# Retention in a fused kernel: one chunk per visit in every group, or two chunks in every second group

## The chip, the cores and the metric

One core of a Trainium2 chip runs the kernel. The metric is the device time of one execution in microseconds; the median of three runs of the kernel before is 662.99 us (662.89 to 663.08).

## The reference, cut to what matters

A retention layer runs over q, k, v of shape (4, 8, 768, 64): batch, heads, time, head dimension. Its output, rearranged to 3072 tokens of 512, goes through a feed-forward block with 2048 hidden columns.

```python
for t in range(S):
    state = gamma[None, :, None, None] * state + np.einsum('bhd,bhe->bhde', k[:, :, t], v[:, :, t])
    y[:, :, t] = scale * np.einsum('bhd,bhde->bhe', q[:, :, t], state)
x = y.transpose(0, 2, 1, 3).reshape(B * S, H * D)
h = x @ w_in
sp = np.maximum(h, 0.0) + np.log1p(np.exp(-np.abs(h)))
out = (h * erf(sp)) @ w_out
```

## The kernel before, in words

**Retention in chunks.** Time is cut into chunks of 128 steps: 6 per batch, 24 in all, numbered j (j % 6 is the place in the batch). Keys and queries are scaled by powers of gamma, so that the state needs no decay between chunks. A chunk needs its scores (keys times queries inside each half chunk of 64 steps), the causal mask on them, the masked scores times the values, the old state times the queries, the crossed part of the second half, and two additions to the state, one per half chunk. Heads are 64 wide, so all of these are 64x64 matmuls, which use the quadrants of TensorE's array; all else on TensorE is 128x128.

**The feed-forward block.** The first 512 tokens (groups g = 0 to 3, `hidden` at L865, `project` at L885) are computed in the plain way, while the weights are still being converted from 64-bit words. From group G0 = 4 on the work goes by 256 tokens, two groups to each: g - G0 even and odd hold the two halves of the hidden columns. Group G0 takes the plain product (`hidden_plain`, L971); the groups from G0+1 to G0+19 use a scheme with 26 products in place of 32 for the hidden columns (`hidden_steps`, L942: 26 steps of two matmuls, whose results VectorE and ScalarE add up from four PSUM banks, two named hp and two named r) and 7 in place of 8 for the output (`project_part`, L1022). The scheme wants sums of x (`x_sums`, L921: 18 VectorE operations for each 256 tokens), sums of weights (`W_SUMS`, `sums` at L347, whose additions are DMAs issued by POOL) and sums of the gated values (`g_sums`, L1004).

**The order of a group** is written out by hand in the loop at L1224. Each engine executes its part in this order. TensorE does the 26 steps of group g with products 1, 2 and 4 of group g-1 set behind steps 14, 18 and 24; then a visit to the retention, `sub_visit` (L713), one chunk in each group from G0 (j = 6) to G0+17 (j = 23); then products 5, 6, 7 and 3 of group g-1. ScalarE computes softplus of the hidden values, copies the visit's results to xT, then computes erf. VectorE does the additions and masks of the visit, then x_sums (in odd groups) or the preparation of a chunk (in even ones, `prepared` at L533: scale the keys, scale and transpose the blocks of keys and queries), then the gate `gated` (L846), h times erf. The results of a pair of groups are added up and written out in the next odd group (`put_part`, L1048, from four PSUM banks o0 to o3).

**A visit** (L713 to L797) multiplies the old state with the queries, adds the products of keys and values for both half chunks into two banks (`adds`), multiplies values with the masked scores, straight and crossed, makes the scores of the next chunk, and then multiplies the state after the first half with the queries. VectorE adds to the state between (L777) and behind (L797). Chunk 6 is an exception: its scores and its first half's addition are made in the middle of `hidden_plain` (`sub_begin`, L708).

**Transfers.** `load` (L192) brings a chunk's keys in rows, its queries and keys once more as blocks that VectorE can transpose (`load_blocks`, L181: 16 transfers each) and its values: 34 transfers, all issued by SP, behind the visit. The results of the first 512 tokens go out through SP too (`put_first`, L907).

Of the kernel before, what the change touches and what calls it, by code (L numbers as in the profile page):

```python
# [19 lines left out]
P = 128  # L20
C = 128
# [115 lines left out]
def kernel(  # L137
# [39 lines left out]
    KQ, V, KB = {}, {}, {}  # L177
# [3 lines left out]
    def load_blocks(to, src):  # L181


        for s, d in itertools.product(range(2), range(2)):
            part = slice((2 * s + d) * 32, (2 * s + d + 1) * 32)
            for u in range(HP):
                nc.sync.dma_start(
                    to[part, u * C : (u + 1) * C].rearrange("p (a d) -> p a d", d=32),
                    src[2 * u + s, :, d * 32 : (d + 1) * 32].rearrange("(a p) d -> p a d", p=32),
                )  # L190

    def load(j):  # L192
        b, c = divmod(j, NC)
        if j == JPC - 1:

            x = act.tile([P, N], F32, name="e", bufs=1)
            KQ[j] = x[:, : 2 * d_model].rearrange("p (i h d) -> p i h d", i=2, h=H)
            V[j] = x[:, 2 * d_model : 3 * d_model].rearrange("p (h d) -> p h d", h=H)
        else:
            KQ[j] = loads.tile([P, 2, H, D], F32, name="kq")  # L200
            V[j] = loads.tile([P, H, D], F32, name="v")
        now = slice(c * C, (c + 1) * C)
        if j >= NB:
            KB[j] = loads.tile([P, HP * C], F32, name="kb", bufs=2)
            nc.sync.dma_start(KQ[j][:, 0], k[b, :, now, :].rearrange("h p d -> p h d"))
            load_blocks(KQ[j][:, 1].rearrange("p h d -> p (h d)"), q[b, :, now, :])
            load_blocks(KB[j], k[b, :, now, :])
        for i, src in enumerate((k, q) if j < NB else ()):
            nc.sync.dma_start(KQ[j][:, i], src[b, :, now, :].rearrange("h p d -> p h d"))
        if not early:  # L210
            load_values(j)

    def load_values(j):
        b, c = divmod(j, NC)
        nc.sync.dma_start(V[j], v[b, :, c * C : (c + 1) * C, :].rearrange("h p d -> p h d"))

# [214 lines left out]
    state_2 = loads.tile([P, HP * C], F32, name="kb", bufs=2)[:, : HP * D]  # L431
    state_2 = state_2.rearrange("p (u d) -> p u d", d=D)
    mid = [state, state_1, state_2, state, None, state_1]
    adds_of = {JPC: range(2), JPC + 1: range(1), JPC + 2: range(1)}
# [97 lines left out]

    def prepared(j):  # L533

        if j >= NJ:
            return
        nc.vector.tensor_tensor(
            KQ[j][:, 0], KQ[j][:, 0],
            kq_s[:, j % NC, 0, :, None].to_broadcast([P, H, D]), op=ALU.mult,
        )  # L540
        yield
        blocks = (KB[j], KQ[j][:, 1].rearrange("p h d -> p (h d)"))
        for i, x in enumerate(blocks):
            x = x.rearrange("p (u a d) -> p u a d", u=HP, d=32)
            by = kq_b[:, j % NC, i, :, :, None].to_broadcast([P, HP, 4, 32])
            nc.vector.tensor_tensor(x, x, by, op=ALU.mult)
            yield
        for name, store, x in zip("kq", (KT, QT), blocks):
            store[j] = ret.tile([P, HP, C], F32, name=name + "T")
            nc.vector.transpose(store[j].rearrange("p u t -> p (u t)"), x)  # L550
            yield
# [161 lines left out]
    def sub_visit(j, g):  # L713
# [8 lines left out]
        pp = [ret_psum() for _ in range(2)]  # L722
# [7 lines left out]
        def of_state(a):  # L730
            t = slice(a * D, (a + 1) * D)
            for u in PAIRS:
                for r in range(2):
                    col, own = u // 2, slice(r * D, (r + 1) * D)
                    x = state_1 if g == G0 else state
                    nc.tensor.matmul(  # L736
                        pp[r][col * D : (col + 1) * D, u % 2, t], x[own, u, :], QT[j][own, u, t],
                        start=first(r, col), stop=True, skip_group_check=True,
                    )

        other = SC[j + 1] = [ret_psum(ps_h) for _ in range(2)]

        def of_values(crossed):
            for u in PAIRS:
                for a in range(2):
                    r = 1 - a if crossed else a
                    col, t = u // 2, slice(a * D, (a + 1) * D)
                    own = slice(col * D, (col + 1) * D)  # L750
                    nc.tensor.matmul(  # L751
                        other[a][own, u % 2, D:] if crossed else pp[a][own, u % 2, t],
                        V[j][t, 2 * u + r, :],
                        AM[j][t, r, u, :D],
                        start=crossed or first(r, col), stop=True, skip_group_check=True,
                    )

        if c:
            of_state(0)
        last = chunk_of(g - 1)  # L760
        if (g - G0) % 2 == 1:
            clear.update((("o", 0), ("o", 1)))
        new = [
            None if g == G0 else O[last][3][:, 1, :].rearrange("p (u d) -> p u d", d=D),
            pp[1][:, 2:, :].rearrange("p a (b d) -> p (a b) d", d=D),
        ]
        adds = range(int(g == G0), 2 if c < NC - 1 else 1)
        for u in range(HP):
            for r in range(2):
                for a in adds:  # L770
                    t, h = slice(a * D, (a + 1) * D), 2 * u + r
                    nc.tensor.matmul(  # L772
                        new[a][r * D : (r + 1) * D, u, :], KQ[j][t, 0, h, :], V[j][t, h, :],
                        start=first("o" if a == 0 else 1, r), stop=True, skip_group_check=True,
                    )
        if g > G0 and c:
            nc.vector.tensor_tensor(state, state, new[0], op=ALU.add)  # L777
        elif g > G0:
            nc.vector.tensor_copy(state, new[0])
        of_values(False)  # L780
        of_values(True)
        if j + 1 < NJ:
            sub_scores(j + 1)
            sub_mask(j + 1)
        of_state(1)
        for r in range(2):
            a = 1 - r
            x, y = XC[m][:, r::2, i * C : (i + 1) * C], other[a][:, :2, D:]
            if c or a:
                nc.scalar.copy(x, pp[r][:, :2, :])  # L790
                x = x[:, :, a * D : (a + 1) * D]
                nc.vector.tensor_tensor(x, x, y, op=ALU.add)
            else:
                nc.scalar.copy(x[:, :, D:], pp[r][:, :2, D:])
                nc.scalar.copy(x[:, :, :D], y)
        if c < NC - 1:
            nc.vector.tensor_tensor(state, state_1 if g == G0 else state, new[1], op=ALU.add)  # L797
# [109 lines left out]
    def put_first(tt):  # L907
        o = E[G0 - 1].rearrange("p (u t c) -> p t u c", u=FG, t=TT)[:, tt]
        nc.scalar.copy(o, O[0][tt].rearrange("p (u c) -> p u c", u=FG))
        nc.sync.dma_start(out[tt * P : (tt + 1) * P, :].rearrange("p (u c) -> p u c", u=FG), o)  # L910
# [109 lines left out]
    HOME = {2: (0, 0), 6: (0, 1), 5: (1, 0), 7: (1, 1), 3: (2, 0), 4: (2, 1), 1: (3, 0)}  # L1020

    def project_part(g, p, at=slice(None)):  # L1022
# [7 lines left out]
        i, half = (3, 1) if p == 4 and g >= NG - 2 else HOME[p]  # L1030
# [17 lines left out]
    def put_part(m, step):  # L1048


        o26, o57, o34, o1 = (O[m][i] for i in range(4))
        if step == 0:
            R[m] = act.tile([P, 8, DH], F32, name="r", bufs=1)
            nc.scalar.copy(R[m][:, 7], o1[:, 0])
            return
# [11 lines left out]
        else:  # L1067
            nc.vector.tensor_tensor(r[:, 1:3], r[:, 5:7], o34, op=ALU.add)
# [37 lines left out]
    def next_scores():  # L1106
# [37 lines left out]
            ([(load, 6), (sub_results, 5)], []),  # L1144
            ([(load, 7)], [(sub_sums, 5)]),
# [40 lines left out]
    j = JPC + 2  # L1186
    sum_in(1, 12)
    all_of(prepared(j))
    load(j + 2)
    gated(G0 - 1)  # L1190
    for n, _ in enumerate(hidden_plain(G0), start=1):
        if n in (1, 4, 7):
            next(last_steps)
        if n == 3:
            sub_begin(j)
    sum_in(1, 20)
    x_sums(G0)
    sub_states(j)
    all_of(prepared(j + 1))
    sum_in(1, len(W_SUMS))  # L1200
# [3 lines left out]
    sub_visit(j, G0)  # L1204
    load(j + 3)
# [3 lines left out]
    sum_in(0, 12)  # L1209
    for tt in range(1, TT):  # L1210
# [4 lines left out]
    j += 1  # L1215
# [8 lines left out]
    for g in range(G0 + 1, NG):  # L1224
# [6 lines left out]
        next_chunk = prepared(j + 1) if even or put is None else iter(())  # L1231

        if put is not None:
            order = {18: (e_sums,), 20: (e_sums,), 24: (e_sums, e_sums)}
        else:
# [4 lines left out]
        if g == G0 + 1:  # L1240
            order.update({n: (w_sums,) for n in (1, 2, 3, 4)})
# [12 lines left out]
        all_of(next_chunk)  # L1254

        nc.scalar.activation(idle, idle, AF.Softplus)
        gate_softplus(g)
        if more:
            sub_visit(j, g)
        all_of(w_sums)  # L1260
        if g == G0 + 1:
            all_of(last_steps)
        if g + 1 < NG and not even:
            x_sums(g + 1)
        if more:
            if even:
                all_of(prepared(j + 2))
            if j + 3 < NJ:
                load(j + 3)
            j += 1  # L1270
        gate_erf(g)
        for p in (5, 6, 7, 3):
# [77 lines left out]
```

## Time and profile before

| what | value |
|---|---|
| median of 3 runs | 662.99 us |
| the profiled execution | 662.78 us |
| its span, first to last instruction | 660.9 us |
| granted TensorE clock | 1.00 |
| TensorE matmul busy | 655.7 us, 6200 instructions |
| VectorE busy | 508.4 us |
| ScalarE busy | 280.2 us |
| transfers | 51.88 MB, 159413 packets |

The span runs from the first to the last instruction; 1.9 us of the execution lie around it. A float32 matmul call of the kernel stands as two instructions in the trace. A row of the timeline names start, length, engine, line, operation, tiles, shape and number of instructions; idle time ahead of it and what ended that stand in brackets. A matmul's length there includes its way through the array; how fast matmuls follow one another is read from their starts. The hidden stages of the groups G0+1, G0+2, G0+3 begin at 158.41, 184.32 and 210.25 us, that of the last group at 622.07 us.

### The profile page before, as it was taken

The numbers are of one execution on the slowest core, as the hardware profiler recorded it, in microseconds if no ns is written. First come the engines' busy times: TensorE is split into PE (matmuls) and PEld (weight loads), VectorE is DVE, ScalarE is ACT, GpSimd is POOL, SyncE is SP. The second block draws the span as 40 slices with busy tenths as digits, with TensorE's granted clock in tenths as the row PEclk, the third lists the DMA queues.
The fourth block names the chain that finished last, engine by engine and source line by source line (L and its number), as shares of the span: only waits on it lengthen the run. The fifth ranks groups of instructions, "written<-read, shape, count | busy, mean of one in ns | idle before, by whom it ended". The sixth has DMA issues, their size and how long they took to land.

```text
span 660.9 us, 15247 instructions
## 1 busy us (share of the span) xinstructions
PE 655.7 (99%) x6200; PEld 557.3 (84%) x6200; DVE 508.4 (77%) x1102; ACT 280.2 (42%) x402; POOL 11.7 (2%) x29
## 2 busy tenths in 40 slices
PE   8999999999999999999999999999999999999998
PEld 7744444576999999999999999999999999999997
DVE  5999999969986786788678678677687688476464
ACT  3468363445534334244254253342432542533440
POOL 1000000110100000000000000000000000000000
PEclk9999999999999999999999999999999999999999
DMA  9999844385753321222222322221231210000000
GB/s 188 223 264 231 211 129 107 63 152 90 144 123 61 85 47 32 67 47 46 70 44 47 73 39 46 42 72 37 44 79 36 46 53 1 2 34 0 1 33 32
DMA packets 159413, 51.88 MB, mean 78 GB/s; under 512 B 143216, under 2 KB 149744, under 8 KB 159344
## 3 DMA queue, kind: packets, MB, share of 16 engines
q1 hardware_dynamic: 157776, 46.72, 32.8%
q0 software_dynamic: 1152, 4.19, 3.4%
q8 instruction: 48, 0.79, 0.5%
q14 instruction: 21, 0.17, 0.1%
q10 hardware_dynamic: 416, 0.01, 0.0%
HBM read 40.39 MB, written 6.29 MB: 71 GB/s over the span
## 4 chain that ended last, share of the span: by engine, by line
PE 98%; DMA 1%; DVE 0%; ACT 0%; issue 0%
PE o L1034 37%; PE hp L951 22%; PE r L951 12%; PE hp L860 8%; PE o L896 8%; PE hp L980 2%; PE r L736 2%; PE hp L628 1%; PE o L772 1%; PE r L524 1%; PE r L557 1%; PE o L604 1%; PE r L751 1%; PE hp L751 1%; DMA kq<-in_k_dram 1%; PE r L772 0%
## 5 line engine op out<-in xcount | busy, mean ns | idle before, releaser
L1034 PE MATMUL o<-w_out_sb,h 128*128 128x256 f32 (+1 forms) x640 | 142.7, 380 | 0.0
L951 PE MATMUL hp<-xs,w_in_sb 128*128 128x128 f32 x988 | 138.1, 275 | 0.0
L1034 PEld LDWEIGHTS o<-w_out_sb,h 128*128 128x128 f32 x640 | 119.5, 190 | 16.6
L963 DVE TENSOR_TENSOR h<-h,hp 128x256 f32<-128x256 f32 x190 | 78.0, 418 | 70.5 <-PE hp L951 65.6
L951 PEld LDWEIGHTS hp<-xs,w_in_sb 128*128 128x128 f32 x988 | 128.4, 192 | 3.0
L1034 PE MATMUL o<-w_out_sb,e 128*128 128x256 f32 x480 | 113.5, 379 | 0.0
L1034 PEld LDWEIGHTS o<-w_out_sb,e 128*128 128x128 f32 x480 | 86.8, 190 | 9.4
L817 ACT ACTIVATE e<-h 128x2048 f32<-128x2048 f32 x22 | 42.1, 1912 | 119.6 <-DVE h L963 119.6
L963 DVE TENSOR_TENSOR h<-h,r 128x256 f32<-128x256 f32 x152 | 56.9, 415 | 22.3 <-PE r L951 21.4
L965 ACT COPY h<-hp 128x256 f32<-128x256 f32 x38 | 14.2, 373 | 130.7 <-PE hp L951 122.7
L951 PE MATMUL r<-xs,w_in_sb 128*128 128x128 f32 x456 | 63.3, 275 | 0.0
L951 PEld LDWEIGHTS r<-xs,w_in_sb 128*128 128x128 f32 x456 | 57.0, 192 | 0.0
L860 PE MATMUL hp<-xT,w_in_sb 128*128 128x512 f32 (+2 forms) x144 | 56.5, 548 | 0.0
L849 DVE TENSOR_TENSOR e<-h,e 128x1024 f32<-128x1024 f32 x42 | 49.2, 1213 | 8.0 <-ACT e L830 8.0
L860 PEld LDWEIGHTS hp<-xT,w_in_sb 128*128 128x128 f32 x144 | 25.8, 190 | 27.0 <-issue 24.6
L951 PE MATMUL hp<-xT,w_in_sb 128*128 128x128 f32 x304 | 46.3, 275 | 0.0
L951 PEld LDWEIGHTS hp<-xT,w_in_sb 128*128 128x128 f32 x304 | 41.5, 192 | 1.4 <-issue 0.5
L830 ACT ACTIVATE e<-e 128x2048 f32<-128x2048 f32 (+1 forms) x23 | 42.1, 1836 | 0.2
L967 ACT ACTIVATE h<-hp 128x256 f32<-128x256 f32 x57 | 21.9, 384 | 29.7 <-PE hp L951 28.3
L951 PE MATMUL r<-xT,w_in_sb 128*128 128x128 f32 x228 | 31.7, 275 | 0.0
L830 ACT ACT_TABLE_LOAD x24 | 30.8, 1283 | 0.4
L951 PEld LDWEIGHTS r<-xT,w_in_sb 128*128 128x128 f32 x228 | 28.5, 192 | 0.0
(164 smaller groups left out, 799.0 us busy)
## 6 DMA issues: line engine op xcount, KB each, us to landing
w_out_sb<-in_moe_w_out_dram SPq DMA_DIRECT2D x14, 512.0 KB, 5.2
kq<-in_k_dram SPq DMA_DIRECT2D x23, 256.0 KB, 4.0
v<-in_v_dram SPq DMA_DIRECT2D x23, 256.0 KB, 3.4
out_dram<-r SPq DMA_DIRECT2D x23, 256.0 KB, 2.9
kq<-in_q_dram SPq DMA_DIRECT2D x288, 16.0 KB, 1.9
kb<-in_k_dram SPq DMA_DIRECT2D x288, 16.0 KB, 1.8
w_in_sb<-in_moe_w_in_dram SPq DMA_DIRECT2D x8, 512.0 KB, 10.1
w_out_sb<-w_out_sb POOLq DMA_DIRECT2D x8, 512.0 KB, 5.3
```

Of the source, the lines that this page charges most:

```text
L736: nc.tensor.matmul(pp[r][col * D : (col + 1) * D, u % 2, t], x[own, u, :], QT[j][own, u, t], start=first(r, col), stop=True, skip_group_ch ...
L751: nc.tensor.matmul(other[a][own, u % 2, D:] if crossed else pp[a][own, u % 2, t], V[j][t, 2 * u + r, :], AM[j][t, r, u, :D], start=crossed ...
L817: nc.scalar.activation(E[g], HS[g], AF.Softplus)
L830: nc.scalar.activation(E[g][:, half], E[g][:, half], AF.Erf)
L849: nc.vector.tensor_tensor(E[g][:, half], HS[g][:, half], E[g][:, half], op=ALU.mult)
L860: nc.tensor.matmul(HP_[ft][:, t], w_in_of(ft, kk), XC[0][:, kk, t], start=(kk == 0), stop=(kk == n_k - 1),)
L896: nc.tensor.matmul(O[0][tt].rearrange("p (d c) -> p d c", d=2), E[g][:, u * TCH + tt * P : u * TCH + (tt + 1) * P], w_out_of(ft), start=(f ...
L951: nc.tensor.matmul(to[:, u, :], w_in_sb[:, s, w, u * P : (u + 1) * P], XS[m](x), start=first and u == 0, stop=True, skip_group_check=True,)
L963: nc.vector.tensor_tensor(h, h, of, op=ALU.add if plus else ALU.subtract)
L965: nc.scalar.copy(h, of)
L967: nc.scalar.activation(h, of, AF.Copy, scale=-1.0)
L1034: nc.tensor.matmul(O[m][i][:, half, at], G[g][a][:, u * P : (u + 1) * P], w_out_sb[:, s, OUT[b], u, at], start=i not in started, stop=(s = ...
```

## The change

- `sub_visit` becomes `pair_visit`, which handles chunks j and j+1 and runs in odd groups only, nine times. It makes all additions of keys and values for both chunks first, into two r banks, then the products with the old state, the values, the scores of chunk j+2, and then, one half chunk after the other, the products with the states that VectorE has added up meanwhile (four states in a ring, `states`), the scores of chunk j+3 and the last crossed products. Its results lie in the banks o1 and o2.
- The scores of chunks 6 and 7 are made alone in group G0 (`pair_scores`), those of 8 and 9 in G0+2. `sub_begin(6)` inside `hidden_plain` goes.
- `load` is split. `load_turned` brings the blocks (32 transfers) into two buffers in turn, `load_pair` the keys and values of two chunks (4 transfers) behind the pair visit. The blocks of keys of chunks 10 and 11 are issued by POOL, all others by SP.
- The keys of a pair are scaled by one VectorE operation, `key_scale`; `prepared` keeps four of its five operations. Even groups prepare chunks; G0+3, an odd one, prepares chunk 11 between its hidden steps.
- Product 4 shares bank o3 with product 1, which ScalarE copies together; products 6 and 5 change places; the first results go out through POOL.

```diff
+    def load_turned(j):
...
+        for i, src in enumerate((k, q)):
+            queue = nc.gpsimd if j in (JPC + 6, JPC + 7) and i == 0 else nc.sync
+            load_blocks(BLOCKS[j][:, i], src[b, :, c * C : (c + 1) * C, :], queue)
...
+    def pair_scores(j):
+        to = banks_of(ps_r)
+        for i in range(2):
+            turned_scores(j + i, [x[:, i] for x in to])
...
+    def pair_visit(j, scores):
...
+        pp = [ps_o.tile([P, 2, 2, 2, D], F32, name=f"o{r + 1}") for r in range(2)]
...
+        new = [ret_psum(ps_r).rearrange("p (i a) (b d) -> p i (a b) d", i=2, d=D) for _ in range(2)]
+        adds = range(4 if c + 2 < NC else 3)
+        for i, u, r, a in itertools.product(range(2), range(HP), range(2), range(2)):
+            if 2 * i + a in adds:
+                t, h = slice(a * D, (a + 1) * D), 2 * u + r
+                nc.tensor.matmul(
+                    new[a][r * D : (r + 1) * D, i, u], KEYS[j][t, i, h, :], V[j + i][t, h, :],
+                    start=first("new", a, r), stop=True, skip_group_check=True,
+                )
         if c:
             of_state(0)
...
+        of_values(False)
+        mixed = [ps_h.tile([P, 2, HP, D], F32, name="hp") for _ in range(2)]
+        other = [x[:, 0].rearrange("p (i a) d -> p i a d", i=2) for x in mixed]
+        if scores:
+            turned_scores(j + 2, [x[:, 1] for x in mixed])
+        of_values(True, (1,))
+        for n in adds:
+            x, to = states[n], states[(n + 1) % 4]
+            i, a = divmod(n, 2)
+            if c or n:
+                nc.vector.tensor_tensor(to, x, new[a][:, i], op=ALU.add)
+            else:
+                nc.vector.tensor_copy(to, new[a][:, i])
+            of_state(n + 1) if n < 3 else None
+        if scores:
+            turned_scores(j + 3, [x[:, 0] for x in banks_of(ps_r)])
+        of_values(True, (0,))
...
+        if scores:
+            pair_mask(j + 2)
...
-        nc.sync.dma_start(out[tt * P : (tt + 1) * P, :].rearrange("p (u c) -> p u c", u=FG), o)
+        nc.gpsimd.dma_start(out[tt * P : (tt + 1) * P, :].rearrange("p (u c) -> p u c", u=FG), o)
...
-        next_chunk = prepared(j + 1) if even or put is None else iter(())
+        next_chunk = iter(())
+        if g == G0 + 1:
+            next_chunk = prepared(j + 2)
+        elif g == G0 + 2:
+            next_chunk = prepared(j + 1)
+        elif g == G0 + 3:
+            next_chunk = prepared(j + 3)
+        elif even:
+            next_chunk = prepared(j + 2)
...
+        if g == G0 + 2:
+            load_turned(j + 3)
...
-        if more:
-            sub_visit(j, g)
+        if more and not even:
+            pair_visit(j, g > G0 + 1 and j + 2 < NJ)
+        elif g == G0 + 2:
+            pair_scores(j)
...
+            load_turned(j + 4)
...
+            if j + 2 < NJ:
+                load_pair(j + 2)
+            if g > G0 + 1:
+                load_turned(j + 5)
+            j += 2
...
+            load_turned(j + 4)
+            if g > G0 + 2:
+                all_of(prepared(j + 3))
+            key_scale(j)
         gate_erf(g)
-        for p in (5, 6, 7, 3):
+        for p in (6, 5, 7, 3):
             project_part(g - 1, p)
```

## The prediction

> **What bounds the kernel now.** I read the page first: sections 1 and 4.
>
> ```profile
> span 660.9 us, 15247 instructions
> ...
> PE 655.7 (99%) x6200; PEld 557.3 (84%) x6200; DVE 508.4 (77%) x1102; ACT 280.2 (42%) x402; POOL 11.7 (2%) x29
> ...
> PE 98%; DMA 1%; DVE 0%; ACT 0%; issue 0%
> ```
>
> TensorE is busy for 99% of the span and is 98% of the chain that ended last. So only two things can move the time: what TensorE itself spends, and a wait that reaches it. The list of waits has, after the start-up, no TensorE wait over 0.8 us, and one wait for the retention state: 0.2 us, once, in the last visit. So I look for time inside TensorE's own stream, around a visit (timeline; columns: start, us, engine, line, operation, tiles, count).
>
> ```profile
> 381.87 0.61 PE L951 MATMUL hp<-xT,w_in_sb 128*128 128x128 f32 x4
> 382.41 0.46 PE L736 MATMUL r<-qT,state 64*64 64x64 f32 x16
> ...
> 383.16 0.41 PE L751 MATMUL r<-am,v 64*64 64x64 f32 x16
> 383.39 0.42 DVE L777 TENSOR_TENSOR state<-state,o 128x256 f32<-128x256 f32 x1 [0.45 <-PE r L772]
> 383.39 0.41 PE L751 MATMUL hp<-am,v 64*64 64x64 f32 x16
> 383.62 0.65 PE L628 MATMUL hp<-qT,kT 64*64 64x64 f32 x32
> 384.09 0.41 PE L736 MATMUL r<-qT,state 64*64 64x64 f32 x16
> 384.43 1.99 PE L1034 MATMUL o<-w_out_sb,h 128*128 128x256 f32 x8
> ```
>
> The trace shows two instructions for each matmul call. 32 small ones take 0.47 us (383.62 to 384.09), so 14.6 ns each, four quadrants side by side. A visit has 128: 1.87 us. Its edges cost more: the four 112 ns matmuls from 381.87 end at 382.32, but the visit starts at 382.41; its last 16 small ones need 0.23 us, but L1034 comes 0.34 us after them. The whole price comes from a group with a visit against one without (TensorE's timeline):
>
> ```profile
> 365.52 0.61 PE L951 MATMUL hp<-xT,w_in_sb 128*128 128x128 f32 x4
> ```
>
> ```profile
> 598.37 0.61 PE L951 MATMUL hp<-xT,w_in_sb 128*128 128x128 f32 x4
> ...
> 622.07 0.61 PE L951 MATMUL hp<-xT,w_in_sb 128*128 128x128 f32 x4
> ```
>
> The group from 365.52 lasts until 391.44, 25.92 us; that from 598.37 has no visit and lasts 23.70 us. The difference is 2.22 us, of which 1.87 is work: **each block of 64x64 matmuls costs 0.35 us for entering and leaving**, whatever its length. The first block (132.56 to 133.96) gives 0.35 too.
>
> **The change, part by part.**
>
> 1. *Fewer blocks.* Before, from the first group on a half chunk: `sub_begin(6)` and 18 visits, 19 blocks. After: nine pair visits, and `pair_scores` alone at G0 and at G0+2, 11 blocks. Eight go: 8 x 0.35 = **-2.8 us**. The small matmuls themselves stay the same in number.
>
> 2. *Chunk 6.* Before, its key-value products are made in two blocks, each with one half of the rows (`adds` holds one value). Such a series uses two quadrants of four and runs at half the rate: the visit at 278.97 has 112 small instructions and lasts 2.02 us like those of 128, where that at 304.88, with 112 of the other kind, lasts 1.79. So 16 instructions of one row half cost 0.47 us and not 0.23. After, both halves alternate in one block: 2 x 0.23 = **-0.5 us**.
>
> 3. *The chain of states in a pair visit.* VectorE now makes up to four dependent additions (0.42 us each, L777) where it made one or two, and TensorE needs each result. From the visit's start S: 64 instructions of additions end at S+0.98 (with the 0.05 us that the first four lose); the first VectorE addition starts 0.27 us after the last issue, as at 383.12 to 383.39; so results at S+1.66, 2.08, 2.49 and 2.91, and TensorE goes on 0.05 us later, as in the last visit (addition over at 590.91, L736 at 590.97). TensorE meanwhile does old state (0.23), values (0.47), scores (0.47), crossed values (0.23): it asks at S+2.38, 2.62, 2.85, and at S+3.08 for the bank that the fourth addition empties. Spare: 0.67 to 0.12 us, no wait. Without the scores and old state (first pair) it asks at S+1.68, 1.94, ...: up to 0.4 us lost, nothing if the first half's products release the addition alone; I take **+0.2**. The last pair, also without scores: 0 to 0.15 us, where the last visit now loses 0.2: **-0.1**.
>
> 4. *After a pair visit.* TensorE has 7.0 us of products (384.43 to 391.44) before it wants the next hidden stage. S+3.8 ends the visit, so S+10.9. VectorE and ScalarE have to copy (two of about 0.58, L878's shape), add the crossed values (2 x 0.42), mask four times (1.5), make the x sums (386.04 to 390.18, 4.1) and the gate (2.35): done about S+12.9. Hidden's first VectorE operation comes 2.5 us after hidden's start (391.44 to 393.95), at S+13.4. Today that place has 1.42 us of idle VectorE, then 0.5: hidden, at 0. If that cover goes, the four banks still let TensorE run some 1.8 us (four steps of 0.45). The product order 6, 5 costs nothing: product 5 needs bank o1, copied by S+4.0, at about S+4.7.
>
> 5. *Groups without a visit.* They get four operations of `prepared` (0.60 each as they follow at 412.57 to 414.99, 2.4) and `key_scale` (1.22, the 128x1024 row of L514): 3.6 us. The cover is the wait for the error function:
>
> ```profile
> 621.04 2.36 DVE L849 TENSOR_TENSOR e<-h,e 128x1024 f32<-128x1024 f32 x2 [5.26 <-ACT e L830]
> ```
>
> In a group without a visit VectorE idles 5.26 us there. 0. The put of results has one copy and one addition more per pair, under 0.5 us of engines that wait for TensorE: 0.
>
> 6. *Transfers.* That they leave the visits is worth nothing by these rows (us, busy by engine, clock, DMA share, GB/s):
>
> ```profile
> 175.29:177.31 2.02, 2.02 (x129) 1.96 (x128) 1.03 (x4) 1.40 (x1) 0.00 (x0) 1.00 1.10 203
> ...
> 253.05:255.07 2.02, 2.02 (x129) 1.96 (x128) 1.03 (x4) 1.40 (x1) 0.00 (x0) 1.00 0.00 0
> ```
>
> A visit under full DMA lasts as long as one without any. SP issues the same 34 transfers per chunk, at 0.43 to 0.55 us each some 17 to 19 us, two chunks in 51 us. In the steady state the pieces queue in this order: keys and values (4) behind the visit that frees their buffer, then the odd chunk's 32 blocks, done about S+25, wanted at about S+28; then the even chunk's, wanted over 20 us after. Behind a late one stands the gate, with 1.2 us spare before part 4's cover: 0.
>
> 7. *POOL.* `put_first` (4) and the key blocks of chunks 10 and 11 (2 x 16) move there. The only transfers that POOL issues before:
>
> ```profile
> L353 POOL DMA_DIRECT2D w_out_sb<-w_out_sb x8 | 7.0, 878 | 54.2 <-ACT w_out_sb L352 42.0 <-PE r L951 6.5 <-PE hp L980 5.6
> ```
>
> A block of 128 pieces has as many rows as those. Hidden of G0+2 and G0+3 start at 184.32 and 210.25 now, by parts 1 to 3 at about 183.4 and 208.5. At 0.86 us, chunk 10's keys are issued behind the last sum (179.61 now) from about 179 to 193, chunk 11's from 194.5, when step 18 of G0+2 has freed the buffer (18 x 0.45, product 1 and some lag behind 183.4), to 208.3, landed by 210 (1.8 us, SP's blocks) or 213.6 (5.3 us, L353's). VectorE wants them at step 10 of G0+3, 10 x 0.45 behind 208.5: about 213. Cost 0, bounds: SP's 0.43 us each and SP's slowest 2.07. I take 0.86, the row of the same engine. The four sums at POOL wait behind `put_first` at most some us; ScalarE, which waits for them, has no copy to make then.
>
> One rule speaks against this part. The Trainium skill, "GPSIMD Engine Reference", section 8, says that GpSimd shares its SBUF interfaces with VectorE and contends with VectorE instructions that have two SBUF inputs. The row: between 160 and 175.8 us VectorE is busy 14.06 of 15.80 us, much of it with such instructions, and the POOL issues there take 0.85 us, as in quieter places. By the row nothing is lost; by the rule each issue could wait for an addition to end, which would lead to the slower rival below.
>
> **Sum** against the profiled execution: span 660.9 - 2.8 - 0.5 + 0.2 - 0.1 = 657.7, and 1.9 around it: 659.6 (it took 662.78). The median is 0.2 above that execution, so **659.8**.
>
> **Rivals.**
>
> *A. The chain of states replaces the edges.* For it: four dependent additions, the fourth with 0.12 us spare. Against: VectorE is free at S+0.6, well before S+1.24. If VectorE came 0.5 us later, each of nine visits would lose about 0.35 us, 3.2 in all, which gives the gain back: 662 to 663.5. Chance 0.08.
>
> *B. POOL is slow, and VectorE stands at the scaling of chunk 11 in G0+3.* For it: no 16 KB issue of POOL in the trace, and 3 us spare at most. With c us per issue the keys land at 179 + 32c + 1.8; VectorE stands from 213; TensorE follows about 3.5 us later, when steps 11 to 14 and product 1 are used up. It decides from c = 1.1; c = 1.26 costs 4.6 us and the kernel is slower than before; c = 1.5 costs 12 us, 672. Range 664 to 672. Against: 0.85 to 1.01 in eight rows. Chance 0.07.
>
> *C. The edges are not all saved*: the two blocks of scores alone and waits inside pairs keep half of the 3.2 us: 661 to 662. Chance 0.10. That the edges belong to a block, not to its length, is what the 0.35 at blocks of 48 and 128 speaks for.
>
> *D. More is saved*, if the cost counted from matmul to matmul (0.40 per block) is right: 659.0 to 659.4. Chance 0.10.
>
> **The numbers.** Forecast 659.4 to 661: 0.65. A measurement tells 0.2%, 1.3 us, from no change, so faster means under 661.7: forecast, D and most of C, 0.83; same: the rest of C and A, 0.10; slower: 0.07, B. The range 659.0 to 662.8 leaves out B, part of A, and a little below.
>
> **What would show it.** Blocks of 64x64: 11 from G0-1 on. Groups without a visit 23.7 us, with a pair about 27.8 (25.92 + 1.87). No TensorE wait for `state` over 0.2 us save in the first pair. In the windows of G0+3 no VectorE wait for a DMA. Wrong if TensorE's idle time shows at step 14 or 15 of G0+3, if pairs last over 4.3 us, or if the wait at the gate reaches hidden's first steps.

## The result and the profile after

| | us |
|---|---|
| kernel before, median of 5 runs | 662.95 (662.89 to 663.08) |
| changed kernel, median of 5 runs | **672.26** (670.54 to 673.89) |
| ratio, 95% interval | 1.0141 [1.0129, 1.0152] |
| changed kernel, profiled execution and its span | 670.54 and 668.2 |
| span forecast | 657.7 |

The change makes the kernel 1.4% slower. The profiled execution is the fastest of the five. TensorE's own work is unchanged ("after" stands for the changed kernel; this is its page):

```profile
span 668.2 us, 15366 instructions
...
PE 656.1 (98%) x6200; PEld 557.6 (83%) x6200; DVE 507.0 (76%) x1087; ACT 282.1 (42%) x384; POOL 32.0 (5%) x65
...
PE 97%; issue 1%; DMA 1%; DVE 0%; SPq 0%; ACT 0%; DVEq 0%
```

"issue" on the chain has gone from 0% to 1%: TensorE standing with nothing that the profile sees it wait for. The list of the waits of TensorE's matmuls (engine, line, what was waited for; us in total, times, longest) says where. Before, it had no such row:

```profile
PE o L780 <- issue: 4.2, 3, 2.3
...
PE r L740 <- issue: 1.3, 2, 0.7
PE hp L791 <- issue: 1.0, 2, 0.6
```

All three lines are inside `pair_visit`, or in the scores that it calls. The timeline of the visit for chunks 14 and 15 ("the pair of chunks 14 and 15" from here on) shows one such stop:

```profile
386.24 1.16 PE L803 MATMUL r<-v,kq 64*64 64x64 f32 x64
...
388.62 0.41 PE L780 MATMUL o<-qT,state 64*64 64x64 f32 x16
388.86 0.39 PE L780 MATMUL o<-qT,am 64*64 64x64 f32 x10
390.26 0.51 PE L780 MATMUL o<-qT,am 64*64 64x64 f32 x20 [1.01 <-issue]
...
391.46 0.48 PE L1081 MATMUL o<-w_out_sb,h 128*128 128x256 f32 x1
```

L780 multiplies a state that has been ready since the first ten of these matmuls. It goes on for 22 more, but stops among them, in the middle of one loop. Measured from matmul start to matmul start the stop is 1.22 us. The pair after it has none. The two as windows (us, then busy time by engine, clock, DMA share, GB/s):

```profile
386.24:391.46 5.22, 4.21 (x258) 4.01 (x257) 2.19 (x6) 2.52 (x3) 0.00 (x0) 1.00 0.28 64
439.05:442.93 3.88, 3.88 (x241) 3.82 (x240) 1.77 (x5) 2.48 (x3) 0.00 (x0) 1.00 0.04 10
```

Over the nine pairs the stops are 2.55, 0.96, 1.10, 0.81, 1.22, 0, 0.77, 0.63 and 0 us: **8.0 of the 10.5 us** by which the span exceeds the forecast. The group around the pair of chunks 16 and 17, which has no stop, lasts 27.78 us; 27.8 was forecast.

**What the stops have in common.** I counted TensorE's records (matmuls, weight loads and its sequencer's) from the start of the program. Every one of the seven stops falls on record 190 or 191 modulo 256. And each ends 1.3 to 1.5 us after a packet of the queue that carries instructions. For the stop above, in the window from 387.8 to 388.9 us (queue, kind: packets, MB, share):

```profile
q8 instruction: 1, 0.02, 5.2%
```

It is the only transfer there: it starts at 387.93, takes 0.92 us, and the stop ends at 390.26. The pages of before and of after both have this row:

```profile
q8 instruction: 48, 0.79, 0.5%
```

That is one packet of 16 KB for every 256 of TensorE's some 12490 records, 64 bytes for each. The run e5 below adds 2048 TensorE instructions, and its page shows 56 packets.

**Theory F, code loading.** TensorE's program comes in pieces of 256 instructions. By the packets' starts in slow and in fast stages, a piece is asked for about 288 instructions before its first is due, and is usable some 3.4 us later: about 1 us until the packet starts, 0.9 to 1.4 on its way, 1.4 until the first instruction runs. These 288 instructions last 16 us in the hidden stage (55 ns each) and 31 us in the products (108 ns), but only 2.1 us in a block of 64x64 matmuls (7.3 ns each: 14.6 ns for a matmul and its weight load). A visit of before has 256 instructions, so request and first use never lie in one block. A pair visit has 352 to 512, and they can. By the count above, exactly the seven pairs that stop hold both the first instruction of a piece and the place 288 ahead of it; those of chunks 16 and 22 do not.

The Trainium skill, "Runtime: NRT & Kernel Launch", section "Instruction fetch mechanics", says that instructions are refilled in blocks of 16 KiB, 256 instructions, and that crossing a boundary is mostly hidden. The size agrees with the 48 packets here. Hidden it is in the 55 and 108 ns stages; it isn't at 7.3 ns, by the stops above.

**Rivals.** The stops belong to the pair visit itself (its order, its chain of states, more instructions of one kind in a row than some queue can take); or to the transfers of keys, queries and values that now run at other times (called D below).

### The profile page after: what moved, and what is told of

It reads as the page before. It is cut to its first block, busy times and chain, and to the rows that moved or that the text cites. A ratio compares the mean times of both kernels' runs of the same rounds, so it can differ in the third digit from the quotient of the medians.

```text
span 668.2 us, 15366 instructions
## 1 busy us (share of the span) xinstructions
PE 656.1 (98%) x6200; PEld 557.6 (83%) x6200; DVE 507.0 (76%) x1087; ACT 282.1 (42%) x384; POOL 32.0 (5%) x65
## 4 chain that ended last, share of the span: by engine, by line
PE 97%; issue 1%; DMA 1%; DVE 0%; SPq 0%; ACT 0%; DVEq 0%
PE o L1081 36%; PE hp L998 22%; PE r L998 11%; PE hp L907 8%; PE o L943 8%; PE hp L1027 2%; PE r L803 1%; PE o L780 1%; PE r L740 1%; DMA kq<-in_k_dram 1%; PE hp L791 1%; PE r L578 1%; PE o L625 1%; PE o L791 1%; PE r L543 1%
```

## The experiments

Each ratio is to the kernel before on the same chip, with its 95% interval. The runs follow in their order; the output of e4 is not the reference's.

| run | median us | ratio |
|---|---|---|
| e1_aligned | 666.24 | 1.0054 [1.0035, 1.0073] |
| e2_misaligned | 671.13 | 1.0129 [1.0109, 1.0149] |
| e3_split | 668.03 | 1.0079 [1.0059, 1.0098] |
| e4_no_transfers | 671.48 | 1.0131 [1.0114, 1.0148] |
| e5_scores_thrice (the kernel before) | 688.11 | 1.0382 [1.0368, 1.0397] |
| e6_late_sums | 673.80 | 1.0163 [1.0149, 1.0177] |
| e7_aligned_late_sums | 669.69 | 1.0117 [1.0099, 1.0135] |
| e8_split_by_product_4 | 673.87 | 1.0168 [1.0153, 1.0184] |
| e9_early_sums | 670.41 | 1.0105 [1.0091, 1.0120] |
| e10_aligned_early_sums | 664.26 | 1.0021 [1.0010, 1.0031] |

**e1 and e2: the same work, the pieces' borders moved.** Empty TensorE instructions, spread evenly over the hidden steps, shift where the requests fall; only the numbers differ between the two.

```diff
+    PADS = {1: 102, 3: 88, 5: 135, 7: 154, 9: 139, 11: 136, 13: 154, 15: 139}   # e1
+    PADS = {1: 102, 3: 15, 5: 122, 7: 154, 9: 152, 11: 123, 13: 154, 15: 152, 17: 73}   # e2
...
+        for _ in range(n):
+            nc.tensor.nop(hint="pad", nofuse=True)
```

> Theory F (code loading): TensorE's stream of instructions arrives in pieces of 256; a pair visit of 480 to 512 instructions that follow each other every 7.3 ns runs out of them, because the next piece is asked for 288 instructions ahead (2.1 us) and takes about 3.4 us. Here 1047 empty instructions are spread over TensorE's hidden steps, where matmuls take 112 ns, so that the request falls 22 to 36 instructions ahead of each pair visit. F expects the idle stretches of 0.6 to 2.5 us inside the visits to go (under 0.3 us left in each, the waits for the state in the first and the sixth pair aside), pairs of about 3.9 us and a time of 659 to 662 us, if empty instructions hide behind the matmuls; what they cost if not, the next kernel shows. Rival D (transfers of data hold up the visit) and rival V (VectorE's chain of additions): the idle stretches stay, about 1 us in seven pairs, and the time stays at 672 us or rises by the empty instructions.

> The same number of empty instructions, but placed so that the request falls 50 instructions into each of the pair visits from the second on. F: every one of the seven pairs from the second to the eighth stands still for about 1.2 us at the same place, instruction 338 of the visit (matmul 169 of the trace's block), so 8 to 9 us more than with the aligned ones. D and V: no difference between the two.

Measured: 666.24 and 671.13. From the second pair to the eighth theory F holds. With e1's borders the largest stop is 0.43 us and the seven groups sum to 197.1 us; with e2's each pair stops for 1.0 to 1.5 us and they sum to 203.9. e2's waits from 216 us on are one row, all on the line with instruction 338 of the visit, where the expectation put them:

```profile
PE o L780 <- issue: 7.5, 7, 1.3
```

The difference of the medians is 4.9 and not 8 to 9 us, since the first pair goes the other way: there the two kernels are the same, and yet it stops for 3.48 us in e1's profile and 1.39 in e2's. Here is e1's stop, and TensorE's clock after it (windows; the clock is the last but two):

```profile
178.13 0.39 PE L791 MATMUL hp<-am,v 64*64 64x64 f32 x10 [3.26 <-issue]
```

```profile
178.20:179.60 1.40, 1.40 (x73) 1.40 (x73) 0.00 (x0) 0.09 (x1) 0.00 (x0) 0.69 0.27 46
179.60:180.60 1.00, 1.00 (x16) 0.79 (x9) 0.42 (x1) 1.00 (x4) 0.00 (x0) 0.50 0.12 17
```

For 3.4 us, until 182.1, TensorE has half its clock. The first pair's group lasts 31.79 us; e2's, 28.11, makes 26.7 without its stop, so e1 loses 5.1 us here. The packet that it waits for started at 175.84 in e1 and at 173.64 in e2; the place 288 instructions ahead was passed at 168.4 in both. In the hidden steps before the visit, POOL's additions of output weights (512 KB each) are on their way until 176 us, from 170 on at a DMA share of 1.0 to 1.1. So the expectation for e1 was 5 us too low by the first pair, and a second question arose: does the packet wait behind these transfers?

**e3: each pair cut in two by a product of the group's end.**

```diff
+            turned_scores(j + 2, [x[:, 1] for x in mixed], range(2))
+        project_part(g - 1, 6)
+            turned_scores(j + 2, [x[:, 1] for x in mixed], range(2, HP))
...
         for p in (6, 5, 7, 3):
+            if p == 6 and more and not even:
+                continue
```

> Pair visits with product 6 (four 128x256 matmuls, 1.7 us) moved into their middle, behind half of the scores. F: no stretch of small matmuls has over 256 instructions, so no idle stretch over 0.3 us; the nine added entries and exits cost 9 x 0.35 = 3.2 us: 662 to 664 us. D: idle stretches stay, 674 to 676 us. V: product 6 gives VectorE 1.7 us more, so they go too: 662 to 664 us.

Measured: 668.03. The halves have at most 256 instructions, and no stop is left but one of 1.29 us in the first pair, in a half of 160 instructions: its packet started at 176.57, behind the same transfers. In the other pairs the stops need a long block. Alone, e3 doesn't rule out the chain of states, since product 6 also gives VectorE more time; e1 and e2, which have the same chain, do. But the time is 4 us above what I expected. The missing product was cover: the groups without a visit last 23.88 to 23.99 in place of 23.70 us, since VectorE is still at the gate (239.92 to 242.27 in one of them) when TensorE wants the first bank of the hidden steps read, and TensorE waits 0.2 us for it; 1.8 us over seven groups. The first pair's stop and the last pair's second edge (27.73 in place of 27.10) are most of the rest.

**e4: no transfers of keys, queries, values and blocks from chunk 12 on.** The early buffers are used again.

```diff
         BLOCKS[j] = TURNED[j % 2]
+        if j >= 12:
+            return
...
+            V[j + i] = V[j + i - 2] if j >= 12 else loads.tile([P, H, D], F32, name="v")
+        if j >= 12:
+            return
```

> The changed kernel without the transfers of keys, queries, values and blocks from chunk 12 on; old data are used again and scaled by 1, so the output is not the reference's. F: the five idle stretches from 330 us on stay where they are, 0.6 to 1.2 us each: 671 to 673 us. D: they go, 4 us less: 667 to 668 us. V: they stay.

Measured: 671.48, as F has it. The pairs stop at the same chunks, for 0.92, 1.09, 0, 0.62 and 1.21 us, with a DMA share of 0.03:

```profile
386.38:391.46 5.08, 4.21 (x258) 4.00 (x257) 2.19 (x6) 2.57 (x3) 0.00 (x0) 1.00 0.03 6
542.83:548.03 5.20, 4.21 (x257) 4.00 (x257) 2.18 (x6) 2.57 (x3) 0.00 (x0) 1.00 0.03 6
```

Rival D falls for the pairs from chunk 12 on.

**e5: long blocks in the kernel before.**

```diff
-            sub_scores(j + 1)
+            for _ in range(3 if g > G0 else 1):
+                sub_scores(j + 1)
```

> The kernel before, whose visits are 224 to 256 TensorE instructions long, with the scores of the next chunk computed three times over in each of the 16 visits that compute them: 64 more calls, 256 more instructions in each, so that a visit holds 352 to 384 without any other part of the change. The work itself is 64 calls of 2 x 14.6 ns, 1.87 us a visit, 29.9 us in all. Theory F (code loading: a piece of 256 instructions is asked for 288 instructions ahead of its first and is there some 3.4 us later, while 288 small instructions last 2.1 us): six visits hold both the request and the piece's first instruction, by the instructions counted in the built program those of chunks 9, 12, 13, 16, 19 and 20; each of them stands still some 1.2 us with nothing waited for, the other ten do not; 662.9 + 29.9 + 7 = 700 (698 to 702). Rival (the stops belong to the pair visit itself, to its order of products or its states): no stops, 693 (692 to 694).

Measured: 688.11. Two things in the expectation were miscounted. The scores are 16 calls, not 32, so 32 calls are added, 128 instructions and 0.94 us a visit (2.96 us in place of 2.02), 15.0 in all: F should have said 685 and the rival 678. And the visits with threefold scores begin with chunk 7, not 6, so the six that I named by their place in the list are those of chunks 10, 13, 14, 17, 20 and 21. The count of the records in e5's own trace gives the same six: no other visit holds both a piece's first instruction and the place 288 ahead of it. Exactly these six stop, at the same place modulo 256 as above, for 1.54, 1.30, 1.08, 1.44, 0.77 and 1.24 us, 7.4 us; the other ten last 2.73 to 2.96 us. Two neighbours (windows, without and with a stop) and the stop itself:

```profile
233.12:236.08 2.96, 2.96 (x194) 2.89 (x193) 1.04 (x4) 1.91 (x1) 0.00 (x0) 1.00 0.23 54
259.97:264.57 4.60, 3.27 (x193) 3.07 (x193) 1.06 (x4) 1.91 (x1) 0.00 (x0) 1.00 0.33 70
```

```profile
263.95 0.39 PE L628 MATMUL hp<-qT,kT 64*64 64x64 f32 x11 [1.33 <-issue]
```

Behind the visit of chunk 7 TensorE stops 2.1 us in a product, again at a piece's first instruction, with the DMA engines' share at 1.06, and then has half its clock for 3.4 us. The group is 3.9 us longer for it; with 15.0 and 7.4 that makes some 689. **Six places read off the program's layout, in a kernel that has nothing else of the change, are the strongest evidence for F**, though the numbers of the expectation were wrong; the rival that the stops belong to the pair visit falls.

**e6: three of the weight sums moved out of the first pair's window, to the next group.**

```diff
-            order.update({n: (last_steps,) for n in (11, 17, 23)})
+            order[11] = order.get(11, ()) + (last_steps,)
+        if g == G0 + 2:
+            for n in (1, 8, 15):
+                order[n] = order.get(n, ()) + (last_steps,)
...
-            all_of(last_steps)
```

> The changed kernel with three of the four sums of output weights that group G0+1 makes (a copy on ScalarE and a 512 KB addition issued by POOL each) moved from the steps 17 and 23 and from behind the first pair visit into the steps 1, 8 and 15 of group G0+2. No TensorE instruction is moved. Theory F with its addition (the piece of code for the first pair visit waits on the DMA rings behind two of these 512 KB transfers, which are on their way from 169 to 176 us): the packet starts about 1.1 us after its request, the stop in the first pair falls from 2.55 to some 1.2 us, the other stops stay: 671 (670 to 671.8). Rival (the first pair's longer stop has another cause): 672.3.

Measured: 673.80, outside both expectations, but the profile separates them. The first pair's stop falls from 2.55 to 0.61 us and its group from 29.75 to 27.81. Its packet starts 0.9 us after the place 288 instructions ahead, where in the changed kernel it took 3.0: it had waited behind these transfers. What lost the time was my move. Product 4 of group G0+2 needs the last of the sums, and now waits for it:

```profile
PE o L1081 <- DMA w_out_sb<-w_out_sb: 3.5, 1, 3.5
```

With half the clock for 3.4 us behind this wait (not 1.4, as the expectation of e9 has it), that group lasts 30.36 us in place of 24.99.

**e7: both cures.** e6's order and e1's empty instructions in other numbers, 1057 in all: `{1: 146, 3: 53, 5: 138, 7: 154, 9: 137, 11: 138, 13: 154, 15: 137}`.

> The changed kernel with both cures: the weight sums as in the run on late sums, and 1045 empty TensorE instructions spread over the hidden steps so that the request for the piece with the visit's second half goes out 130 instructions ahead of the first pair, 48 ahead of those of 480 instructions and 32 ahead of those of 512. Theory F: no stops over 0.3 us in any pair, groups with a pair 27.8 us, the first one near 26.8: span 658.5, time 660.4 (659.3 to 661.8), below the 662.9 of the kernel before, and close to the 659.8 that was predicted for the change. Rival (what the first aligned kernel had above 660 was the empty instructions' own cost, or a loss that no supply of code explains): 664 to 666 as there.

Measured: 669.69, outside both expectations. The first pair has no stop for code (its group 27.25 us). Group G0+2 loses 5.4 us as in e6. And I had placed the border of the pairs of 512 instructions badly: the next piece begins right behind the pair, and its request, 288 instructions earlier, is still inside. So each of the three stops at the first product behind it:

```profile
393.17 1.02 PE L1099 MATMUL o<-w_out_sb,h 128*128 128x256 f32 x4 [1.36 <-issue]
```

That is F once more, against my own placing.

**e8: the cut by product 4 of the same group**, with e6's order of sums.

```diff
-            if n in (14, 18, 24):
+            if n in (14, 18) or n == 24 and not (more and not even):
...
+        project_part(g - 1, 4)
```

> The changed kernel with the weight sums as in the run on late sums and each pair visit cut in two halves of at most 256 instructions by product 4, which is taken from its place behind step 24 of the same group (in the run on the split by product 6, that product was taken from the end of the group, where it covered the wait of the next group's first steps: 23.99 in place of 23.70 us). No empty instructions. Theory F: no stops over 0.3 us in the pairs, groups without a visit 23.70, and one more edge of 0.35 us in each of nine pairs: 658.5 + 3.2 = 661.7 span, 663.5 (662.5 to 665), no gain over the kernel before. Rival (the split does not cure the stops, or product 4 is missed at its old place): 667 or more.

Measured: 673.87, a miss. No pair has any stop, and the groups without a visit are back at 23.70 us, as expected. But the groups with the pairs of chunks 10 to 21 last 28.69 to 28.92 us, where 27.78 and one edge make 28.13, and the waits have new rows:

```profile
PE hp L1001 <- DVE h L1013: 5.4, 9, 1.0
PE o L1084 <- DMA w_out_sb<-w_out_sb: 2.2, 1, 2.2
```

At its old place behind step 24 product 4 gave VectorE time to empty the banks of the hidden steps. Without it step 25 waits in each of the nine groups, 0.6 us on average. The rest is the late sums again (G0+2: 29.19 us).

**e9 and e10: the sums earlier instead, without and with empty instructions** (`{1: 146, 3: 44, 5: 147, 7: 154, 9: 128, 11: 147, 13: 154, 15: 128}`).

```diff
-            order.update({n: (last_steps,) for n in (11, 17, 23)})
+            for n in (3, 10):
+                order[n] = order.get(n, ()) + (last_steps,)
```

> The changed kernel with the four weight sums of group G0+1 moved off the first pair's window in the other direction: two of them in the steps 3 and 10 (in place of 11, 17 and 23), the other two behind the first visit, so that product 4 of group G0+2 has its operand in time (in the run on late sums it waited 3.5 us for it and TensorE then ran at half its clock for some 1.4 us). No TensorE instruction is moved. Theory F: the stop in the first pair 0.6 to 1.2 us in place of 2.55, the group behind it 25.0 as in the changed kernel, the other stops as before, each 0.8 to 1.5 us by chance of the transfer: 670.5 (669.5 to 671.5). Rival (the first pair's longer stop has another cause than these transfers): 672.3.

> The same early weight sums, and 1046 empty TensorE instructions spread over the hidden steps, so that the request for the next piece of code goes out 130 instructions ahead of the first pair, 48 ahead of the pairs of 480 instructions and 23 ahead of those of 512 (at 32, in the aligned run with late sums, the following piece began with the first instruction behind the pair and TensorE stood still there for 1.6 to 1.8 us). Theory F: no stop over 0.5 us in or behind any pair, the first group with a pair 27.2 us, the others 27.8 to 28.1, groups without 23.70 and 24.99: span 659, time 660.8 (659.8 to 662.2), 0.1 to 0.5% below the kernel before. Rival (the empty instructions or something not seen cost what the removed stops gave): 664 to 667.

Measured: e9 670.41, in F's range, and the first pair's stop is 1.06 us. But that the time agrees is luck: the profile doesn't show the gain. ScalarE now waits 3.0 us for the transfer of the first sum, ahead of results of the hidden steps, and TensorE waits for VectorE there:

```profile
PE hp L998 <- DVE h L1010: 0.9, 2, 0.6
```

The hidden stage lasts 1.7 us longer up to the visit (18.5 us, 16.9 in the changed kernel), and so the first pair's group lasts 29.91 us, no less than the 29.75 of the changed kernel. The profiled spans are 669.3 and 668.2.

e10: 664.26, over 12 runs from 662.9 to 666.0, above F's range and at the lower edge of the rival's; 8 us below the changed kernel and still 0.2% above the kernel before. All waits that the list shows for its TensorE from 150 to 640 us:

```profile
PE o L1099 <- issue: 0.4, 1, 0.4
PE hp L740 <- issue: 0.2, 1, 0.2
```

In the profiled run (span 662.2) the pairs of 480 instructions make groups of 27.78, 27.96, 27.78 and 27.96 us, as without stops, with the empty instructions among them: these cost nothing that shows. The pairs of 512 instructions meet two borders: 29.05, 28.66 and 28.18 us, 2.5 us above 27.78, of which some 0.4 lie in the hidden steps of G0+3, as in the changed kernel. The first group, 27.56, is 0.3 above the 27.25 of e7. Taken off, these 2.4 us would make a span of 659.8. That is a sum, not a run, and 2 us above the span that was forecast: no version here beat the kernel before.

## Why the prediction was wrong

**The step that failed** is the reading behind the first fences: "each block of 64x64 matmuls costs 0.35 us for entering and leaving, whatever its length". It was checked on blocks of 48 to 128 matmuls, 256 instructions at most, and used for blocks of 352 to 512. Up to 256 it holds, save where a packet is held up (e3's first pair). Above, a block can contain both the request for a piece of code and the piece's first instruction, and stands still for 0.6 to 1.5 us, for 2.5 or 3.5 where the packet waits behind other transfers. None of the four rivals named it. It is 8.0 us of the error. A second term was too small, the chain of states (part 3): 8.0 us off the span of 668.2 leaves 660.2, only 0.7 below the 660.9 of before, where 3.2 was forecast. The page of before had the row of the instruction queue, 48 packets, and I passed over it as a transfer that nothing waits for.

By the prediction's parts:

1. *Fewer blocks:* right as far as it goes. Group G0+2, with `pair_scores` alone, lasts 24.99 us, which is 23.70 + 0.35 + 0.94 for its 64 matmuls. The pair without a stop makes 27.78 us where 27.8 was said.
2. *Chunk 6:* not seen by itself. The hidden stage of G0+1 begins at 156.34 us, 2.07 earlier than before; 80 matmuls fewer ahead of it (1.17 us), one edge (0.35) and this term (0.47) make 1.99.
3. *Chain of states:* too small, by 1.4 us. In e10, where these visits have no stop, the pairs of chunks 12 and 18 last 4.07 us each. That of chunk 16 lasts 3.88 without a wait, with 0.23 us more of matmuls, so they lose 0.42 each: they begin a batch and have no old state to multiply, which the part counted for the first pair alone. Reckoned the same way, the first pair (3.30 us, 1.17 less of matmuls) loses 0.59, where up to 0.4 was said and 0.2 taken, and the last (3.20 us, 0.93 less) 0.25, where 0.1 was taken. That is 1.7 us; the sum has 0.3. VectorE's additions follow one another every 0.45 to 0.53 us, where the part took 0.42, in the pair of chunk 12 (after), which starts at S = 333.69:

```profile
334.91 0.42 DVE L821 COPY state<-r 128x256 f32<-128x256 f32 x1 [0.68 <-PE r L803]
335.44 0.42 DVE L819 TENSOR_TENSOR am<-state,r 128x256 f32<-128x256 f32 x1
335.89 0.42 DVE L819 TENSOR_TENSOR am<-am,r 128x256 f32<-128x256 f32 x1
336.35 0.42 DVE L819 TENSOR_TENSOR state<-am,r 128x256 f32<-128x256 f32 x1
```

The fourth ends at S+3.08, where S+2.91 was said. Rival A, 0.35 us in each of nine, came in four pairs only.

4. and 5. *Cover:* right. The eight groups without a visit last 23.70 us in after. e3 and e8 show how thin it is: taking one product out of its place cost 0.2 to 0.6 us a group.
6. *Transfers:* right for the matmuls' pace, and e4 shows that keys and queries have no part in the stops from chunk 12 on. Missed: code is a transfer too. e6 and e9 show that 512 KB additions ahead of the first pair cost it 1.5 to 1.9 us.
7. *POOL:* right, and rival B did not come: in G0+3 VectorE waits for no DMA. The list of POOL's groups in after has its small issues (busy us, mean ns), 0.60 us each, below the 0.86 taken and without the slowdown that rival B needs:

```profile
L187 POOL DMA_DIRECT2D kq<-in_k_dram x32 | 17.6, 600 | 4.7 <-DVE kT L571 3.8 <-DMA w_out_sb<-w_out_sb 0.8
```

**The sum:** 657.7 + 8.0 (stops) + 1.4 (states) = 667.1; the span is 668.2. Of the 1.1 us left, 0.4 lie in G0+3 outside its visit (24.31 us in place of 23.90), which prepares chunk 11 between its steps, and 0.25 behind the start of the last group (39.10 us, before 38.85); the rest I could not place. What stays open is whether F's stops were also part of the spread of the runs of after (670.5 to 673.9, those of before 0.2 us): the packets' times vary by half a microsecond, which fits, but no run separates it. e6's own rise in the pairs of chunks 12 and 18 (1.40 and 1.29 us in place of 0.81 and 0.77) is of that size. The granted clock points to a second part: it was 1.000 in the fastest of these runs and 0.996 and 0.997 in two others, and 0.997 is also the mean in e1's profile, with its 3.4 us at half the clock.

## What to carry to other kernels

Count instructions as well as microseconds. On TensorE, the 288 instructions between the request for a piece of code and its first instruction must last longer than the fetch, here some 3.4 us, or the engine stands still; the profile calls it "issue", and the packets of the instruction queue tell where. The visits of before, of at most 256 short instructions with long ones on both sides, were close to this limit already, and joining two to save an edge of 0.35 us cost two to seven times the edge where a stop came. When steps that depend on each other are joined, look at every place where the work that covered their waits is missing, not only the first. And before an operation is moved out of a tight place, ask what it was covering there, and who needs its result first: five of the ten runs (e3 and e6 to e9) lost gain to that.

## What the runs showed of the hardware

- Counted from the place 288 instructions ahead, a piece of TensorE's code was usable 2.8 to 3.9 us later in the stops of after, e2 and e6 outside the first pair and in the six visits of e5. With bulk transfers at a DMA share of 1.0 to 1.1 it took 5.2 us (after), 7.6 (e2) and 9.7 (e1) in the first pair; moving the transfers (e6, e9) brought 3.3 and 3.7.
- A long stop can cost TensorE its clock. After idle times of 3.3 to 3.5 us (e1, e6, e7) and of 2.0 and 2.2 us (e5, e8) the granted clock was 0.50 for 3.4 us, the same time in all five, and a product's matmuls came every 0.43 us in place of 0.22. After the 2.3 us of the changed kernel (2.55 from start to start) it stayed at 1.00. Which idle time brings it on is open.
- Some 1050 empty instructions on TensorE, up to six to a hidden step, cost nothing that shows: in e1 and e10 groups with them last 23.70 and 27.78 us as without.
